# Attention outputs of batches 1 to 7 turned by DMA transposes instead of on TensorE, and four d_ff chunks of a group begun side by side

## The chip, the cores and the metric

One core of a Trainium2 chip runs the whole kernel. It has a TensorE (PE, whose weight loads are listed as PEld), a VectorE (DVE), a ScalarE (ACT), a GpSimd (POOL), a SyncE (SP) that here only issues DMAs, and 16 DMA engines that all queues share. SBUF and PSUM are on the core; inputs and outputs lie in HBM (device memory). The metric is the device time of one launch in microseconds (us): a median of 327.94 us over three runs before the change, from 324.74 to 328.09.

## The reference

The inputs are q, k and v of 8 batches, 8 heads, 576 positions and 64 columns, and two weight matrices of 512 x 2048 and 2048 x 512. The attention of a head is the sum of two parts. Cut to what matters:

```
q_d, k_d, v_d = means of 4 neighbouring positions      # 144 positions
out_up    = repeat(softmax(q_d k_d^T / 8) v_d, 4)        # each of the 144 rows 4 times
out_local = softmax(q k^T / 8 where |i - j| < 4) v
x = (out_up + out_local) as 4608 tokens x 512            # 512 = 8 heads x 64
h = x @ w_in
out = (h * sigmoid(1.702 h)) @ w_out                     # 4608 x 512, float32
```

## The kernel before

**Tokens and groups.** The second half works on nine groups of 512 tokens (`g`, 0 to 8); a batch has 576 tokens, so batch b must be ready when group g = b begins. `xT[hp]`, four tiles of 128 x 4608 in bf16, hold x transposed: tile hp has the 128 columns of the head pair hp in its partitions, and the tokens along the row. `mm1` makes, for each of the 16 chunks of d_ff (`ffc`), four matmuls of 128 x 512, one for each `xT[dmc]` (`hps_mm`, L704), into one PSUM bank; ACT takes the bank to `gT` by a SiLU (L715). `mm2` makes 64 matmuls for a group (L760), 16 for each of four blocks of 128 tokens; ACT scales each block into `osb` and SP stores it (`store`, L745 and L750).

**Attention among the matmuls.** The attention of batch b is computed during group g = b - 1, cut into steps. The lists `POS` and `POS_0` (group 0) name the places: numbers up to 16 count chunks of `mm1`, and from 16 up, matmuls of `mm2` after the first 16. Step by step: scores of half of the heads on PE (`s_pe`), exponentials on ACT (`s_act`), the same for the other half (`s1`), the products with v for head pairs 0 and 1 and for 2 and 3 (`avn`), and two or four steps `tr`. The order of instructions on every engine is the order in the program (a manual schedule); an engine, or SP's queue, that waits for one instruction holds back all that stand behind it.

**A head pair's output.** `av_local` and `av_down` (L445, L467) write the local and the pooled outputs of a pair, with a column of row sums beside each, into a PSUM tile `PA[n]` of two banks. `normalise` divides on DVE (L483, L484) and leaves `y` with queries in the partitions. `transp` turns `y` by 26 small matmuls with the identity for each pair (L498, L508) into another `PA` tile. `copy_od` (ACT, L617) repeats the pooled part four times, and `merge` (DVE, L638 and L644) adds both and writes `xT[hp]`. Batch 0 goes another way, at the head of the program (`av_local0`, `av_down0`, `normalise0`, `transp_sum`, `copy_x`).

**PSUM.** There are eight banks: three `PA` tiles of two and two single banks `PM`. `mm1` and `mm2` of groups 1 to 8 use the two `PM` banks in turn.

**Loads.** SP's queue holds, in program order, for each group: the rows of v for the pooled part (`load_v4`, L245, six DMAs of 192 KB), the rows of v for the local part (`load_v`, L222, ten DMAs of 128 KB), and the group's four stores. POOL issues the loads of q and k (L202), after the additions that pool q and k (`pool_qk`, L309 and L313), which follow the transposes of q and k on DVE (`prep_1`, L279). In group 0 the loads of batch 2 stand in SP's queue ahead of that group's stores, and the first waits until the last part of `w_out_bf` has landed (the `gate`, L796):

```
            load_v(2, gate=after(w_out_bf[0:1, 12, 0:1], nc.gpsimd))
            load_v4(2)
```

Of the kernel before, what the change touches and what calls it, by code (L numbers as in the profile page):

```python
# [8 lines left out]
FP32 = mybir.dt.float32  # L9
BF16 = mybir.dt.bfloat16  # L10
# [9 lines left out]
def kernel(  # L20
# [9 lines left out]
    nc = tc.nc  # L30
# [33 lines left out]
    eds = [persist.tile([128, 2, 464], BF16, name=f"ed{i}") for i in range(2)]  # L64
# [53 lines left out]
    def fill():  # L118
        nc.vector.memset(wz, 0.0)
        for t in kdT:  # L120
            nc.vector.memset(t[:, SD:160, :], 0.0)
        for t in vbs:
            nc.vector.memset(t[:, :, :, 64:65], 1.0)
        for t in vds:
            nc.vector.memset(t[:, :, :, 64:65], 4.0)
        for t in es:
            nc.vector.memset(t[:, :, 300:304], 1.0)
        for t in eds:
            nc.vector.memset(t[:, :, 432:464], 1.0)
# [300 lines left out]
    def av(b, hp, n=None):  # L430
        o = ps_tile(n)
        av_local(b, hp, o)
        av_down(b, hp, o)
        return o

# [3 lines left out]
    def av_local(b, hp, o, chunks=range(5)):  # L439
        E, vb, o = es[hp], vbs[b % 2], banks(o)  # L440
        for i in chunks:
            for par in range(2):
                for j in range(2):
                    pos = j if par == 0 else 1 - j
                    nc.tensor.matmul(  # L445
                        o[par][64 * pos : 64 * pos + 64, 65 * i : 65 * i + 65],
                        lhsT=E[64 * par : 64 * par + 64, j, 60 * i : 60 * i + 64],
                        rhs=vb[64 * par : 64 * par + 64, i, 2 * hp + j, :],
                        start=True, stop=True,
                        tile_position=(64 * par, 64 * pos),  # L450
                    )

    def av_down(b, hp, o):
        Ed, vd, u, o = eds[hp // 2], vds[b % 2], hp % 2, banks(o)

        blocks = [(kc, x, 0) for kc in range(3) for x in range(2)]
        blocks += [(0, 0, 1), (0, 1, 1), (1, 0, 1), (2, 0, 1)]
        if True:
            for kc, x, c2 in blocks:
                for j in range(2):  # L460
                    pos = j if x == 0 else 1 - j
                    c0 = 65 * (5 + c2)
                    q0 = SD * kc + 48 * (min(x + c2, 1) + x)
                    last = x == c2 == 1
                    if last:
                        q0 = 0
                    nc.tensor.matmul(  # L467
                        o[j][64 * pos : 64 * pos + 64, c0 : c0 + 65],
                        lhsT=Ed[64 * j : 64 * j + 48, u, q0 : q0 + 64],
                        rhs=vd[64 * j : 64 * j + 48, kc, hp, :],  # L470
                        start=(kc == 0), stop=(kc == 2 or last),
                        tile_position=(64 * j, 64 * pos),
                    )

    def normalise(o):
        y = work.tile([128, 2, 7, D], BF16, name="y", tag="y", bufs=4)
        rc = work.tile([128, 2, 7, 1], FP32, name="rc", tag="rc")
        for xs in (slice(0, 1), slice(1, 2)) if o is PM else (slice(0, 2),):
            n = xs.stop - xs.start
            ov = (o[xs.start][:, None, :] if o is PM else o)[:, :, 0:455].rearrange(  # L480
                "p x (c e) -> p x c e", e=65
            )
            nc.vector.reciprocal(rc[:, xs], ov[:, :, :, 64:65])  # L483
            nc.vector.tensor_tensor(  # L484
                out=y[:, xs], in0=ov[:, :, :, 0:D],
                in1=rc[:, xs].to_broadcast([128, n, 7, D]), op=ALU.mult,
            )
        return y

    def transp(y, n=None):  # L490
        x = ps_tile(n)
        for i in range(5):
            for par in range(2):
                for j in range(2):
                    pos = j if par == 0 else 1 - j
                    c0 = 0 if (par == 1 or i == 0) else 3
                    c1 = 60 if (par == 0 or i == 4) else 57
                    nc.tensor.matmul(  # L498
                        x[64 * j : 64 * j + 64, par, 57 * i + c0 : 57 * i + c1],
                        lhsT=y[64 * pos : 64 * pos + 60, par, i, :],  # L500
                        rhs=ident(pos, 60, c0, c1),
                        start=True, stop=True,
                        tile_position=(64 * pos, 64 * j),
                    )
        for c2, xx in ((0, 0), (0, 1), (1, 0)):
            for j in range(2):
                pos = j if xx == 0 else 1 - j
                nc.tensor.matmul(  # L508
                    x[64 * j : 64 * j + 64, xx, 288 + 48 * c2 : 336 + 48 * c2],
                    lhsT=y[64 * pos : 64 * pos + 48, j, 5 + c2, :],  # L510
                    rhs=ident(pos, 48, 0, 48),
                    start=True, stop=True,
                    tile_position=(64 * pos, 64 * j),
                )
        return x

    def av_local0(hp, o, chunks):
        E, vb = es[hp], vbs[0]
        for i in chunks:
            for j in range(2):  # L520
                for par in range(2):
# [7 lines left out]
                    )  # L529

# [16 lines left out]
    def y_tiles0():  # L547
        return (
            work.tile([128, 2, 6, D], BF16, name="yl", tag="yl", bufs=4),
            work.tile([128, 2, 2, D], BF16, name="yd", tag="yd", bufs=4),  # L550
            work.tile([128, 2, 7, 1], FP32, name="rc0", tag="rc0", bufs=4),
        )
# [61 lines left out]
    def copy_od(x):  # L614
        od = work.tile([128, S], FP32, name="od", tag="od")
        for xx, t0, n in ((0, 0, 96), (1, 96, 48)):
            nc.scalar.copy(  # L617
                out=od[:, 4 * t0 : 4 * (t0 + n)].rearrange("p (t f) -> p t f", f=4),
                in_=x[:, xx, 288 : 288 + n, None].to_broadcast([128, n, 4]),
            )  # L620
        return od

    def sub(t, off, *dims):
# [3 lines left out]
        )  # L627

    def merge(b, hp, x, od, eng=None):
        t0 = b * S
        eng = eng or nc.vector
        if eng is nc.gpsimd:
            xs = work.tile([128, 2, 512], BF16, name="xs", tag="xs", bufs=2)
            nc.scalar.copy(out=xs[:, :, 0:288], in_=x[:, :, 0:288])
            x = xs
        eng.tensor_tensor(  # L638
            out=sub(xT[hp], t0 + 3, (57, 2), (114, 5), (1, 57)),
            in0=sub(x, 3, (509, 2), (57, 5), (1, 57)),  # L640
            in1=sub(od, 3, (57, 2), (114, 5), (1, 57)),
            op=ALU.add,
        )
        eng.tensor_tensor(  # L644
            out=sub(xT[hp], t0, (573, 2), (1, 3)),
            in0=sub(x, 0, (512 + 285, 2), (1, 3)),
# [312 lines left out]
```

## Time and profile before

| what | value |
|---|---|
| runs | 324.74, 328.09 and 327.94 us, median 327.94 |
| span of the profiled execution, first to last instruction | 324.8 us (the profile gives no time of its own beside it) |
| PE busy | 312.3 us, 96% |
| ACT, POOL and DVE busy | 184.6, 139.2 and 128.1 us |
| of DVE: divisions of `normalise`, L484 | 28 of 1092 ns |
| of DVE: additions of `merge`, L638 and L644 | 28 of 753 ns and 28 of 169 ns |
| of ACT: copies of `copy_od`, L617 | 56, 18.5 us in all |
| PE work of `transp`, L498 and L508 | 728 small matmuls |
| one group with attention, 98.3 to 131.8 us | 33.5 us, PE busy in all of it |
| a group without, 266.2 to 293.9 us | 27.7 us |

Busy times of several engines overlap, so their sum says nothing. What counts is the chain of work that ended last, and which engine an idle stretch waited for. A matmul of 128 x 512 is listed with 379 ns, but matmuls are pipelined: nine in a row start 0.216 us apart.

### The profile page before, as it was taken

How to read it: one execution, taken by the hardware profiler on the slowest of the kernel's cores; microseconds unless marked ns; L12 is line 12 of the kernel's file. 1: busy time of each engine (PE TensorE's matmuls, PEld its weight loads, DVE VectorE, ACT ScalarE, POOL GpSimd, SP SyncE). 2: the span in 40 equal slices, each digit the busy share in tenths (PEclk: the TensorE clock that was granted, in tenths of full speed). 3: DMA queues.
4: the chain of work that ended last, by engine and by line, in shares of the span. 5: the costliest groups of instructions: out<-in, count | busy, mean ns of one | idle time of the engine just before them, and what ended most of it. 6: DMA issues, size and time to landing. Idle time of an engine off the chain costs nothing.

```text
span 324.8 us, 11101 instructions
## 1 busy us (share of the span) xinstructions
PE 312.3 (96%) x4979; PEld 159.9 (49%) x4979; DVE 128.1 (39%) x221; ACT 184.6 (57%) x321; POOL 139.2 (43%) x171
## 2 busy tenths in 40 slices
PE   7669999899999999999999999999999999999995
PEld 4545455445554555455545554455445544444444
DVE  6864524650566037702780178116720660000000
ACT  4443883375846593659266836774677557415611
POOL 8973960089306950596039802990197000000000
PEclk9988999999999999999999999999999999999999
DMA  7999999799717981699149933994290110021012
GB/s 121 124 202 210 159 122 209 152 249 224 143 69 151 208 162 46 157 199 190 38 130 191 179 90 104 184 193 110 71 141 3 69 48 21 0 84 47 0 60 71
DMA packets 63551, 40.04 MB, mean 123 GB/s; under 512 B 44048, under 2 KB 54416, under 8 KB 63504
## 3 DMA queue, kind: packets, MB, share of 16 engines
q1 hardware_dynamic: 44496, 24.32, 34.4%
q0 software_dynamic: 18864, 14.95, 33.3%
q8 instruction: 39, 0.64, 0.9%
q10 hardware_dynamic: 144, 0.07, 0.1%
q14 instruction: 8, 0.07, 0.1%
HBM read 44.83 MB, written 9.44 MB: 167 GB/s over the span
## 4 chain that ended last, share of the span: by engine, by line
PE 92%; DMA 4%; issue 2%; DVE 1%; POOL 1%; ACT 0%; POOLq 0%
PE pm L704 36%; PE pm L760 36%; PE pa L384 3%; PE pa L403 2%; PE pa L760 2%; PE pa L704 2%; DMA qb<-in_q_dram 2%; PE pa L445 2%; PE pa L498 2%; DMA vb<-in_v_dram 2%; PE pa L467 2%; PE pm L775 1%; PE pm L656 1%; PE pa L508 0%; PE pa L523 0%
## 5 line engine op out<-in xcount | busy, mean ns | idle before, releaser
L760 PE MATMUL pm<-w_out_bf,gT 128*128 128x512 bf16 x528 | 121.7, 380 | 0.0
L704 PE MATMUL pm<-xT,w_in_bf 128*128 128x512 bf16 x544 | 121.1, 379 | 0.0
L715 ACT ACTIVATE gT<-pm 128x512 bf16<-128x512 f32 x136 | 81.0, 598 | 45.6 <-PE pm L704 45.6
L704 PEld LDWEIGHTS <-w_in_bf 128*128 128x128 bf16 x576 | 55.6, 98 | 66.7 <-issue 0.7
L760 PEld LDWEIGHTS <-gT 128*128 128x128 bf16 x560 | 51.6, 98 | 58.5 <-issue 0.2
L309 POOL TENSOR_TENSOR pq<-kT 128x576 f32<-128x576 bf16 x14 | 16.2, 1157 | 90.7 <-DVE kT L279 90.6
L428 DVE TENSOR_TENSOR es<-es,mask 128x600 bf16<-128x600 bf16 x28 | 15.2, 542 | 101.1 <-ACT es L414 99.9
L745 ACT ACTIVATE osb<-pm 128x512 f32<-128x512 f32 (+2 forms) x35 | 20.7, 593 | 41.9 <-PE pm L760 37.9
L617 ACT COPY od<-pa 128x384 f32<-128x384 f32 (+1 forms) x56 | 18.5, 411 | 30.8 <-PE pa L508 26.0
L484 DVE TENSOR_TENSOR y<-pa,rc 128x896 bf16<-128x896 f32 x28 | 30.6, 1092 | 1.0
L638 DVE TENSOR_TENSOR xT<-pa,od 128x570 bf16<-128x570 f32 x28 | 21.1, 753 | 11.0 <-ACT od L617 10.2
L325 POOL TENSOR_TENSOR v<-v 112x512 f32<-112x512 f32 x18 | 22.8, 1265 | 0.0
L747 DVE TENSOR_SCALAR osb<-pm 128x128 f32<-128x128 f32 x1 | 0.3, 292 | 55.3 <-ACT osb L745 55.3
L414 ACT ACTIVATE es<-pa 128x600 bf16<-128x600 f32 x32 | 19.9, 685 | 1.2 <-PE pa L384 1.2
L279 DVE STREAM_TRANSPOSE kT<-kb 128x576 f32<-128x576 f32 x16 | 20.0, 1247 | 0.0
L279 DVE STREAM_TRANSPOSE qT<-qb 128x576 f32<-128x576 f32 x16 | 19.8, 1240 | 0.0
L384 PE MATMUL pa<-qT,kT 32*64 32x60 bf16 x1280 | 16.9, 204 | 1.9 <-DVE qT L279 1.2
L233 POOL DMA_DIRECT2D vb<-in_v_dram x20 | 13.7, 700 | 6.5 <-DMA w_in_bf<-in_moe_w_in_dram 4.0
L384 PEld LDWEIGHTS <-kT 32*64 32x64 bf16 x1280 | 15.0, 103 | 2.6 <-issue 2.0
L420 ACT ACTIVATE ed<-pa 128x864 bf16<-128x864 f32 x16 | 14.4, 903 | 2.3 <-PE pa L403 2.2
L309 POOL TENSOR_TENSOR pq<-qT 128x576 f32<-128x576 bf16 x13 | 14.9, 1146 | 0.0
L328 POOL TENSOR_TENSOR vd<-v 112x256 bf16<-112x256 f32 x18 | 13.8, 769 | 1.4
(97 smaller groups left out, 259.1 us busy)
## 6 DMA issues: line engine op xcount, KB each, us to landing
out_dram<-osb SPq DMA_DIRECT2D x35, 256.0 KB, 2.1
vf<-in_v_dram SPq DMA_DIRECT2D x60, 128.0 KB, 5.8
v<-in_v_dram SPq DMA_DIRECT2D x36, 192.0 KB, 5.2
kb<-in_k_dram POOLq DMA_DIRECT2D x16, 288.0 KB, 7.3
qb<-in_q_dram POOLq DMA_DIRECT2D x16, 288.0 KB, 7.8
w_out_bf<-in_moe_w_out_dram POOLq DMA_DIRECT2D x4, 512.0 KB, 9.9
vb<-in_v_dram POOLq DMA_DIRECT2D x20, 64.0 KB, 5.6
w_in_bf<-in_moe_w_in_dram POOLq DMA_DIRECT2D x2, 512.0 KB, 9.2
```

Of the source, the lines that this page charges most:

```text
L279: nc.vector.transpose(out=t32.rearrange("p (i c) -> p c i", c=18), in_=store[b, qd].bitcast(FP32).rearrange("p (c d) -> p c d", c=18),)
L309: nc.gpsimd.tensor_tensor(out=t1, in0=sv[:, :, 0:2, :], in1=sv[:, :, 2:4, :], op=ALU.add)
L325: eng.tensor_tensor(out=t1[0:112], in0=x[:, :, 0:2, :], in1=x[:, :, 2:4, :], op=ALU.add)
L384: nc.tensor.matmul(sp[r // 2][64 * par : 64 * par + 64, r % 2, 60 * i : 60 * i + 60], lhsT=kT[b, qd][rows, k0 : k0 + 64, a], rhs=qT[b, qd] ...
L414: nc.scalar.activation(out=es[2 * qd + u][:, :, 0:300], in_=sp[u][:, :, 0:300], func=AF.Exp, scale=inv_sqrt_d,)
L484: nc.vector.tensor_tensor(out=y[:, xs], in0=ov[:, :, :, 0:D], in1=rc[:, xs].to_broadcast([128, n, 7, D]), op=ALU.mult,)
L617: nc.scalar.copy(out=od[:, 4 * t0 : 4 * (t0 + n)].rearrange("p (t f) -> p t f", f=4), in_=x[:, xx, 288 : 288 + n, None].to_broadcast([128, ...
L638: eng.tensor_tensor(out=sub(xT[hp], t0 + 3, (57, 2), (114, 5), (1, 57)), in0=sub(x, 3, (509, 2), (57, 5), (1, 57)), in1=sub(od, 3, (57, 2) ...
L704: nc.tensor.matmul(acc, lhsT=w_in_bf[:, dmc, ffc * 128 : (ffc + 1) * 128], rhs=xT[dmc][:, g * TG : g * TG + TG], start=(dmc == 0), stop=(d ...
L715: nc.scalar.activation(out=gT[:, ffc, :], in_=acc, func=AF.Silu, scale=GELU_SCALE)
L745: eng.activation(out=osb, in_=ap, func=AF.Copy, scale=1.0 / GELU_SCALE)
L760: nc.tensor.matmul(ops[t], lhsT=gT[:, ffc, t * 128 : (t + 1) * 128], rhs=w_out_bf[:, ffc, :], start=(ffc == 0), stop=(ffc == n_ffc - 1),)
```

## The change

The change has five parts, for batches 1 to 7.

1. `transp` and its steps go. `turn_y` issues one DMA transpose on SP's queue for each head pair: the whole of `y` (128 x 1024, bf16, 256 KB) into an SBUF tile `x` of eight blocks of 128 x 128. That is 28 DMAs.
2. So that whole blocks can be turned, `y` has another layout. `av_local` and `av_down` write other places of the PSUM tile, in the order that batch 0 had, and `normalise` takes one more instruction. Batch 0 keeps its way and shares the new tile `y`.
3. `copy_od` goes. `merge` is three DVE instructions in place of two: a copy of the local part, a copy of six columns, and an addition of the pooled part, which reads each element four times. The merges of all four pairs stand behind the fourth pair's division.
4. The first four chunks of `mm1` in groups 1 to 8 run side by side: `xT[0]` and `xT[1]` for all four, then `xT[2]`, then `xT[3]`. The chunks are spread over all eight PSUM banks.
5. The places of the steps: the second `avn` comes two matmuls earlier in groups 1 to 6, and in group 0 at 60 in place of 64; batch 1 has five steps as the other batches.

SP's queue in the changed program has, in group 0: ten loads of L222, six of L245, the four transposes of batch 1, and then the four stores. In groups 1 to 6: the loads, the store of block 0, two transposes, the store of block 1, two transposes, and the stores of blocks 2 and 3.

```diff
--- before.py
+++ after.py
-    eds = [persist.tile([128, 2, 464], BF16, name=f"ed{i}") for i in range(2)]
+    eds = [persist.tile([128, 2, 480], BF16, name=f"ed{i}") for i in range(2)]
...
-            nc.vector.memset(t[:, :, 432:464], 1.0)
+            nc.vector.memset(t[:, :, 432:480], 1.0)
...
-    def av(b, hp, n=None):
-        o = ps_tile(n)
-        av_local(b, hp, o)
-        av_down(b, hp, o)
-        return o
...
-        blocks = [(kc, x, 0) for kc in range(3) for x in range(2)]
-        blocks += [(0, 0, 1), (0, 1, 1), (1, 0, 1), (2, 0, 1)]
...
-    def transp(y, n=None):
-        x = ps_tile(n)
-        for i in range(5):
-            for par in range(2):
-                for j in range(2):
-                    pos = j if par == 0 else 1 - j
-                    c0 = 0 if (par == 1 or i == 0) else 3
-                    c1 = 60 if (par == 0 or i == 4) else 57
-                    nc.tensor.matmul(
-                        x[64 * j : 64 * j + 64, par, 57 * i + c0 : 57 * i + c1],
-                        lhsT=y[64 * pos : 64 * pos + 60, par, i, :],
-                        rhs=ident(pos, 60, c0, c1),
-                        start=True, stop=True,
-                        tile_position=(64 * pos, 64 * j),
-                    )
-        for c2, xx in ((0, 0), (0, 1), (1, 0)):
...
+    def av_down(b, hp, o):
+        Ed, vd, u = eds[hp // 2], vds[b % 2], hp % 2
+        blocks = [(kc, c) for kc in range(3) for c in (0, 1)]
+        blocks += [(kc, 2) for kc in range(3)] + [(0, 3)]
+        for kc, c in blocks:
+            pos, slot = ((1, 4), (0, 6), (1, 6), (1, 5))[c]
+            for j in range(2):
+                q0 = SD * kc + 64 * (c % 3)
+                nc.tensor.matmul(
+                    o[64 * pos : 64 * pos + 64, j, 65 * slot : 65 * slot + 65],
+                    lhsT=Ed[64 * j : 64 * j + 48, u, q0 : q0 + 64],
+                    rhs=vd[64 * j : 64 * j + 48, kc, hp, :],
+                    start=(kc == 0), stop=(kc == 2 or c == 3),
+                    tile_position=(64 * j, 64 * pos),
+                )
+
+    def normalise(o):
+        y = work.tile([128, 8, 2 * D], BF16, name="y", tag="y", bufs=4)
+        rc = work.tile([128, 2, 7, 1], FP32, name="rc", tag="rc")
+        ov = o[:, :, 0:455].rearrange("p x (c e) -> p x c e", e=65)
+        nc.vector.reciprocal(rc, ov[:, :, :, 64:65])
+        nc.vector.tensor_tensor(
+            out=y[:, 0:6].rearrange("p (x m) (j d) -> p x (m j) d", x=2, j=2),
+            in0=ov[:, :, 0:6, 0:D],
+            in1=rc[:, :, 0:6].to_broadcast([128, 2, 6, D]), op=ALU.mult,
+        )
+        nc.vector.tensor_tensor(
+            out=y[:, 6:8].rearrange("p s (j d) -> p j s d", j=2),
+            in0=ov[:, :, 4:7:2, 0:D],
+            in1=rc[:, :, 4:7:2].to_broadcast([128, 2, 2, D]), op=ALU.mult,
+        )
+        return y
+
+    def turn_y(y):
+        x = work.tile([128, 8, 128], BF16, name="x", tag="x", bufs=4)
+        nc.sync.dma_start_transpose(out=x, in_=y.rearrange("p g c -> p (g c)"))
+        return x
+
+    def merge(b, hp, x):
+        t0 = b * S
+        nc.vector.tensor_copy(
+            out=sub(xT[hp], t0 + 3, (57, 2), (114, 5), (1, 57)),
+            in_=sub(x, 3, (381, 2), (64, 5), (1, 57)),
+        )
+        nc.vector.tensor_copy(
+            out=sub(xT[hp], t0, (573, 2), (1, 3)),
+            in_=sub(x, 0, (384 + 256 + 57, 2), (1, 3)),
+        )
+        xs = xT[hp][:, t0 : t0 + S].rearrange("p (t f) -> p t f", f=4)
+        nc.vector.tensor_tensor(
+            out=xs, in0=xs,
+            in1=sub(x, 832, (1, SD), (0, 4)), op=ALU.add,
+        )
...
+        y = work.tile([128, 8, 2 * D], BF16, name="y", tag="y", bufs=4)
         return (
-            work.tile([128, 2, 6, D], BF16, name="yl", tag="yl", bufs=4),
-            work.tile([128, 2, 2, D], BF16, name="yd", tag="yd", bufs=4),
+            y[:, 0:6].rearrange("p (x m) (j d) -> p x (m j) d", x=2, j=2),
+            y[:, 6:8].rearrange("p s (j d) -> p s j d", j=2),
             work.tile([128, 2, 7, 1], FP32, name="rc0", tag="rc0", bufs=4),
...
-    def copy_od(x):
-        od = work.tile([128, S], FP32, name="od", tag="od")
-        for xx, t0, n in ((0, 0, 96), (1, 96, 48)):
-            nc.scalar.copy(
-                out=od[:, 4 * t0 : 4 * (t0 + n)].rearrange("p (t f) -> p t f", f=4),
-                in_=x[:, xx, 288 : 288 + n, None].to_broadcast([128, n, 4]),
-            )
-        return od
...
-    def merge(b, hp, x, od, eng=None):
...
-        eng.tensor_tensor(
-            out=sub(xT[hp], t0 + 3, (57, 2), (114, 5), (1, 57)),
-            in0=sub(x, 3, (509, 2), (57, 5), (1, 57)),
-            in1=sub(od, 3, (57, 2), (114, 5), (1, 57)),
-            op=ALU.add,
-        )
...
-    def attention(b, slots=None):
+    def attention(b):
         st = {}
+        slot = (1, 2, 1, 2) if b == 1 else (0, 1, 2, 0)
 
         def s_pe(qd):
-            t = PA if b == 1 else [ps_tile() for _ in range(3)]
-            st["d", qd] = scores_d(b, qd, t[0])
-            st["s", qd] = scores(b, qd, sp=t[1:3])
+            st["d", qd] = scores_d(b, qd, PA[0])
+            st["s", qd] = scores(b, qd, sp=PA[1:3])
 
         def s_act(qd):
             if qd == 0:
@@ -681,24 +621,16 @@
         def avn(*hps):
             def f():
                 for hp in hps:
-                    st["o", hp] = av(b, hp, slots and slots[hp % 2])
+                    av_local(b, hp, PA[slot[hp]])
+                    av_down(b, hp, PA[slot[hp]])
                 for hp in hps:
-                    st["y", hp] = normalise(st["o", hp])
+                    st["x", hp] = turn_y(normalise(PA[slot[hp]]))
+                if hps[-1] == HP - 1:
+                    for hp in range(HP):
+                        merge(b, hp, st["x", hp])
             return f
 
-        def tr(*hps):
-            def f():
-                for hp in hps:
-                    st["x", hp] = transp(st["y", hp], slots and slots[hp % 2])
-                for hp in hps:
-                    od = copy_od(st["x", hp])
-                    merge(b, hp, st["x", hp], od)
-            return f
-
-        first = [lambda: s_pe(0), lambda: s_act(0), s1, avn(0, 1)]
-        if b == 1:
-            return first + [tr(0), tr(1), avn(2, 3), tr(2), tr(3)]
-        return first + [avn(2, 3), tr(0, 1), tr(2, 3)]
+        return [lambda: s_pe(0), lambda: s_act(0), s1, avn(0, 1), avn(2, 3)]
...
-    def mm1(g, gT, steps, first=0):
-        for ffc in range(first, n_ffc):
+    def mm1(g, gT, steps):
+        half = [PA[n][:, u, :] for n in (1, 2, 0) for u in range(2)]
+        bank = [PM[0], *half[0:4], PM[1], *half[4:6]]
+        bank += [PM[0], half[0], half[1], PM[1]] + PM + PM
+        if g == 0:
+            bank = acc[0:6] + late
+        for ffc in range(n_ffc):
             for f in steps.get(ffc, ()):
                 f()
-            hps = pm_tile() if g else acc[ffc] if ffc < 6 else late[ffc - 6]
-            for dmc in range(n_dmc):
-                hps_mm(g, ffc, dmc, hps)
-            silu(gT, ffc, hps)
+            if g and ffc < 4:
+                if ffc == 0:
+                    for dmcs in ((0, 1), (2,), (3,)):
+                        for u in range(4):
+                            for dmc in dmcs:
+                                hps_mm(g, u, dmc, bank[u])
+            elif g or ffc > 5:
+                for dmc in range(n_dmc):
+                    hps_mm(g, ffc, dmc, bank[ffc])
+            else:
+                continue
+            silu(gT, ffc, bank[ffc])
 
     def mm2(g, gT, steps):
         tok0 = g * TG
+        turn["m"] = 1
...
-    POS = [13, 16, 33, 42, 53, 62, 71]
-    POS_0 = [16, 18, 27, 46, 50, 55, 64, 68, 73]
+    POS = [13, 16, 33, 42, 51]
+    POS_0 = [16, 18, 27, 46, 60]
...
-            for n, f in zip(POS if g else POS_0, attention(b, None if g else (1, 2))):
+            for n, f in zip(POS if g else POS_0, attention(b)):
...
-        mm1(g, gT, steps, 0 if g else 6)
+        mm1(g, gT, steps)
```

## The prediction

> **What bounds the kernel now.** I read the page's busy times and chain first, then PE's order of time in one steady group, then SP's queue, because the new DMAs go there.
>
> ```profile
> PE 312.3 (96%) x4979; PEld 159.9 (49%) x4979; DVE 128.1 (39%) x221; ACT 184.6 (57%) x321; POOL 139.2 (43%) x171
> ...
> PE 92%; DMA 4%; issue 2%; DVE 1%; POOL 1%; ACT 0%; POOLq 0%
> ```
>
> PE is the bound, so only PE time and new PE waits count; the 18.5 us of ACT copies that go (L617) lie on no chain and are worth nothing. The end of group 2 on PE:
>
> ```profile
> 124.50 2.12 PE L760 MATMUL pm<-w_out_bf,gT 128*128 128x512 bf16 x9
> 126.55 0.35 PE L498 MATMUL pa<-id,y 60*64 60x60 bf16 x20
> 126.73 0.22 PE L508 MATMUL pa<-id,y 48*64 48x48 bf16 x6
> ...
> 127.10 2.12 PE L760 MATMUL pm<-w_out_bf,gT 128*128 128x512 bf16 x9
> ...
> 129.70 2.12 PE L760 MATMUL pm<-w_out_bf,gT 128*128 128x512 bf16 x9
> 131.66 1.67 PE L704 MATMUL pm<-xT,w_in_bf 128*128 128x512 bf16 x7
> ```
>
> Nine matmuls take 9 x 0.2157 = 1.94 us (a 52-matmul stretch of the chain takes 11.22), so the step `tr` between 124.50 and 127.10 costs 2.60 - 1.94 = 0.66 us, the next one as much, and group 3 starts without a wait. SP's queue in group 0:
>
> ```profile
> 53.24 9.77 SPq L222 DMA_DIRECT2D vf<-in_v_dram  x10
> 63.05 3.06 SPq L245 DMA_DIRECT2D v<-in_v_dram  x6
> 66.23 3.64 SPq L750 DMA_DIRECT2D out_dram<-osb  x4
> ```
>
> The sixteen loads of batch 2 hold the queue until 66.1, after PE has begun group 1 (64.53). The four stores behind them show what a 256 KB DMA meets there, against the median of all stores (the listing for 66 to 70 us, then the page):
>
> ```profile
> out_dram<-osb SPq DMA_DIRECT2D x4, 256.0 KB, 6.5
> ```
>
> ```profile
> out_dram<-osb SPq DMA_DIRECT2D x35, 256.0 KB, 2.1
> ```
>
> **Gain.** For batches 2 to 7, two steps of 0.66 go: 6 x 1.32 = **7.9 us**. In group 0 the four `tr` steps cost 1.96 (gaps of 0.44, 0.43, 0.66 and 0.43), but PE will wait at its end for something that does not depend on them, so I count nothing.
>
> **AV products.** As many matmuls, other order, which batch 0 already has: its 20 L539 took 0.34 us from first load to the next group, 20 L467 took 0.33. I take 0.01 x 28 = **+0.3**. Bounds: nothing to 0.13 a pair (the loads alone, 0.30 against 0.17), 3.6.
>
> **DVE.** Batch 0 has the new division's shapes:
>
> ```profile
> 22.58 0.25 DVE L558 RECIPROCAL rc<-pa 128x14 f32<-128x14 f32 x1 [1.90 <-PE pa L539]
> 22.86 0.42 DVE L560 TENSOR_TENSOR yd<-pa,rc 128x256 bf16<-128x256 f32 x1
> 23.20 0.95 DVE L565 TENSOR_TENSOR yl<-pa,rc 128x768 bf16<-128x768 f32 x1
> ```
>
> 22.58 to 24.15 is 1.57 us a pair, before 1.28. A merge is now two SBUF bf16 passes over about 570 elements and one over six. The mask multiply (L428, SBUF bf16, 600 elements) takes 0.542, so I take 0.54 + 0.54 + 0.12 = 1.2 us. Bounds: 0.88 (the copy at half of it, the small one at 0.07 as the smallest memsets) and 1.67 (two L638 of 0.753 and an L644 of 0.169).
>
> **Steady boundaries (groups 1 to 6).** Let T be the first division, 120.96 in group 2. PE resumes at 121.20, does 9 matmuls, AV (0.93, as in this group) and 29 matmuls: the new group begins at 121.20 + 1.94 + 0.93 + 6.26 = T + 9.37. Side-by-side chunks give 8 matmuls from `xT[0]` and `xT[1]`, then 4 from `xT[2]`, so `xT[3]` is wanted at T + 11.96. Four divisions end at T + 6.28, four merges at T + 11.1: in time by 0.9 us. The fourth turn is issued at T + 6.4 and must land within 11.96 - 6.4 - 1.2 = 4.4 us. The trace has no transpose; a store of equal size lands in 2.1, a v load among its fellows in 5.8. I take 2.1, the nearest in size and quiet: DMAs are idle in most of 121 to 131 us. Cost nothing, covered by those 12 matmuls. At 5.8 it is 1.4 us a boundary, 8.4 in all; at the merge bound of 1.67, merges end at T + 12.96, 1.0 a boundary.
>
> The Trainium skill, "Advanced Engine Details and Errata", section X-Bar Transpose (TRN2), says that these DMAs are as fast as regular ones; by that the 2.1 stands. No run shows it.
>
> **Boundary 0 to 1.** Without its `tr` steps PE ends group 0 at about 62. The turns of batch 1 stand behind the sixteen loads, so the first goes out at 66.2, into rings that are still full: the last v load there, issued at 65.67, took 6.9 us and landed at 72.6, and the first store, issued at 66.23, at 73.3. With a turn in the store's place I take 72.6, since the next q and k loads (POOL, 69.81) now wait behind the merges. Merges end at 73.8, 75.0, 76.2, 77.4; the stores' spacing of 0.8 keeps the later turns ahead of them. PE has then stood still for 11 us, and its clock drops:
>
> ```profile
> 20.00:21.00 1.00, 0.00 (x0) 0.00 (x0) 0.68 (x2) 0.99 (x2) 0.69 (x1) 1.00 1.24 204
> ...
> 23.00:24.00 1.00, 1.00 (x4) 0.40 (x3) 1.00 (x2) 0.00 (x0) 0.80 (x2) 0.50 1.13 213
> 24.00:25.00 1.00, 1.00 (x16) 0.65 (x14) 0.15 (x1) 0.00 (x0) 0.65 (x1) 0.50 1.12 213
> 25.00:26.00 1.00, 1.00 (x44) 0.88 (x43) 0.11 (x1) 0.85 (x3) 0.00 (x0) 0.50 1.12 216
> ```
>
> (granted clock third from the end: about 3.3 us at 0.50 after a pause of some 2 us). So seven matmuls of 0.43 run from 75.0 to 78.0, one more at 0.43, seven at 0.216: the first sixteen end at 79.95. Before, 64.53 + 16 x 0.2157 = 67.98. **Loss 12.0 us.** Without the clock's fall 77.4 + 0.86 = 78.3, loss 10.3; with a first landing as the last one among vf (4.1 after 66.2), 9.7; with one at 2.1, merges of 0.88 and full clock, 68.3 + 3.5 + 0.86, loss 4.7. Behind it queue only DVE's transposes for batch 2, 12 us later, and POOL's chain behind them: 19.4 us from DVE's start to the last `vd` (98.61 to 118.04), wanted some 20 us after the last merge, so just covered. The delayed stores have four `osb` tiles and are wanted a group later.
>
> **Sum.** -7.9 + 0.3 + 12.0 = **+4.4 us**. Span 324.8 becomes 329.2; the page has no own time for the execution, and the lowest run equals the span, so I add to the median: 327.94 + 4.4 = **332.3 us**.
>
> **Rivals.**
> - Slow turns: each lands too late at every boundary as well. For it: DMA rows with 256-byte pieces take 5.8; a queue of four turns at the v loads' rate (1.28 MB in 10.5 us, 2.1 us each) ends at T + 10.1, on the edge. Against: quiet DMAs. 4.4 + 8.4 gives 340.7.
> - Short wait: the rings empty sooner and boundary 0 loses about 7.6, half-way in its bounds: 327.9. Against it speak the four stores' 6.2 to 7.3 us.
> - Faster: the loads of v are out of the way, and the turns hide in group 0 too: -7.9 - 1.96 + 0.3 gives 318.4. It decides if `xT[3]` of batch 1 is whole by about 65. The queue's order speaks against it. That the turns don't replace the matmuls is excluded: the changed program has 28 of them and no L498.
> - A turn by blocks: eight blocks of 128 x 128 one after another, each with the smallest store's landing of 1.6 us, make 12.8 a turn, 51 a batch, more than a group; 66 + 7 x 51 + 58 is 481 us. Against: no DMA row behaves so. The Trainium skill, "VectorE: DVE Perf Modes", section The three transpose paths, gives 1309 ns for such a block against 390 on TensorE; by that a turn would be 10.5 us, by estimate, and the time about 418. No run shows it.
>
> **Chances.** Forecast 0.52 (329 to 335), slow turns 0.22, short wait 0.16, faster 0.08, by blocks 0.02. The measurement tells about 1% from no change, 3.3 us. Of the forecast, 0.40 lies above 331.2 and 0.12 below; short wait gives 0.13 same and 0.03 faster. So faster 0.11, same 0.25, slower 0.64. The range is 326 to 342.5: it leaves out faster and by blocks, and some of slow turns and of short wait.
>
> **What would show it.** No L498 and L508; 128 plain matmuls and 33.5 - 1.3 = 32.2 us in groups 2 to 6 without a PE wait at their starts; in group 0 four transposes on SP at 66 to 70 us, PE idle from about 62 to 74 for DVE's merge, clock 0.50 after it. Wrong if a quiet turn takes over 4.4 us, or if PE waits under 8 us at 62.

## The result, and the profile after

The changed kernel takes **357.63 us** (median of four runs, 356.58 to 359.24), the kernel before 327.43 us beside it (324.74 to 328.09). The ratio is **1.095**, with a 95% interval of 1.088 to 1.102: slower by some 30 us, where +4.4 us were forecast and 342.5 us was the upper end of the range. The profiled execution took 357.70 us, its span is 355.8 us; so a run is its span and 1.9 us, and the span has grown by 31.0 us from 324.8. Medians here and below are over all runs of a kernel; ratios and their intervals leave out the few runs that lay over 1.5% above the kernel's fastest.

The page of the kernel after, first its busy times, then the shares of the chain by engine:

```profile
PE 309.2 (87%) x4251; PEld 154.0 (43%) x4251; DVE 140.8 (40%) x277; ACT 164.1 (46%) x265; POOL 138.4 (39%) x171
...
PE 68%; DMA 8%; ACT 7%; DVE 5%; POOL 4%; SPq 3%; issue 3%; ACTq 0%; POOLq 0%; DVEq 0%
```

PE has the 728 small matmuls less, as the change says, and it is no longer busy all the time: 96% became 87%. On the chain DMA has 8% for 4%, and ACT, which had 0% before, now has 7% of it. ACT itself works less than before (164 for 185 us), so its 7% can't come from its load; something waits for it. The two longest rows of PE's waits say what (line waited for: us in total, times, longest):

```profile
PE pa L636 <- ACT gT L647: 23.4, 24, 1.6
PE pm L636 <- DVE xT L496: 12.4, 2, 11.8
```

The second row is the wait at the end of group 0 that the prediction had. The first is nowhere in the prediction: matmuls of `mm1` (L636) wait for the SiLU (L647), 24 times. In order of time they stand here, in group 3 on PE (start, us, line, operation, count, and in brackets the idle time ahead of it):

```profile
148.87 0.81 PE L636 MATMUL pa<-xT,w_in_bf 128*128 128x512 bf16 x3
149.76 0.38 PE L636 MATMUL pm<-xT,w_in_bf 128*128 128x512 bf16 x1
149.97 0.81 PE L636 MATMUL pa<-xT,w_in_bf 128*128 128x512 bf16 x3
152.35 1.02 PE L636 MATMUL pa<-xT,w_in_bf 128*128 128x512 bf16 x4 [1.56 <-ACT gT L647]
153.21 1.03 PE L636 MATMUL pm<-xT,w_in_bf 128*128 128x512 bf16 x4
154.07 1.03 PE L636 MATMUL pa<-xT,w_in_bf 128*128 128x512 bf16 x4
155.78 1.02 PE L636 MATMUL pa<-xT,w_in_bf 128*128 128x512 bf16 x4 [0.69 <-ACT gT L647]
...
159.22 1.02 PE L636 MATMUL pa<-xT,w_in_bf 128*128 128x512 bf16 x4 [0.69 <-ACT gT L647]
```

and this is ACT in the same microseconds:

```profile
150.73 1.57 ACT L647 ACTIVATE gT<-pa 128x512 bf16<-128x512 f32 x3
...
154.27 0.60 ACT L647 ACTIVATE gT<-pm 128x512 bf16<-128x512 f32 x1 [0.27 <-PE pm L636]
155.14 0.60 ACT L647 ACTIVATE gT<-pa 128x512 bf16<-128x512 f32 x1 [0.27 <-PE pa L636]
```

Three matmul chunks of a group wait, always the same ones. Counted from 0 they are chunks 4, 7 and 10. In the table of banks they are `PA[2]` second half, `PA[0]` second half and `PA[1]` second half, and the chunk just ahead of each has the first half of the same tile. The wait ends when ACT has read that first half: at 152.30 (150.73 + 1.57) ends the SiLU of chunk 3, at 152.35 begins chunk 4; at 155.74 (155.14 + 0.60) ends that of chunk 6, at 155.78 begins chunk 7. Chunk 4 and chunk 3 lie in two different banks; but both are halves of one tile, and the program holds the wait for the whole tile. Its order of instructions on PE shows it: the first matmul of chunk 4 waits for an ACT instruction,

```
Matmult pa2_98<-xT0_79,w_in_bf_77 128x512 [waits Activation_49]
```

and so do the first ones of chunks 7 and 10. Chunks 13 to 15 carry such a wait too, each for the chunk two before it in the same `PM` bank, and chunk 0 one for its bank's last use in the group before; none of these appears among PE's waits, which are the 24 at chunks 4, 7 and 10. Chunk 2 also follows the other half of its tile, but its matmuls stand ahead of all SiLUs of the first four chunks, so it has nothing to wait for.

By the starts of the matmuls a wait costs a little more than the row lists: four matmuls in a row take 0.86 us (152.35 to 153.21). From 149.97 to 152.35, less three matmuls of 0.216, are 1.73; from 154.07 to 155.78, less 0.86, are 0.85, and the third is as long. That is 3.43 us a group, and in the eight groups 1 to 8 **27.4 us** of the 31.0 by which the span grew.

The boundary from group 0 to group 1, on SP's queue:

```profile
50.96 9.77 SPq L222 DMA_DIRECT2D vf<-in_v_dram  x10
60.77 3.05 SPq L245 DMA_DIRECT2D v<-in_v_dram  x6
63.94 8.09 SPq L482 DMA_TRANSPOSE x<-y  x4
72.13 2.01 SPq L696 DMA_DIRECT2D out_dram<-osb  x4
```

and on PE:

```profile
58.01 1.89 PE L706 MATMUL pa<-w_out_bf,gT 128*128 128x512 bf16 x8
71.70 0.61 PE L636 MATMUL pm<-xT,w_in_bf 128*128 128x512 bf16 x1 [11.80 <-DVE xT L496]
72.93 0.58 PE L636 MATMUL pm<-xT,w_in_bf 128*128 128x512 bf16 x1 [0.62 <-DVE xT L496]
...
78.00 1.06 PE L636 MATMUL pa<-xT,w_in_bf 128*128 128x512 bf16 x3
```

The four turns of batch 1 stand behind the sixteen loads of batch 2, the first goes out at 63.94 and lands 6.4 us later, PE stands from 59.9 to 71.7, and the first sixteen matmuls of group 1 end at 78.9. Before, they ended at 67.98: a loss of 10.9 us. The clock falls too, in the windows of two microseconds (the granted clock is the third number from the end):

```profile
66.00:68.00 2.00, 0.00 (x0) 0.00 (x0) 0.00 (x0) 0.00 (x0) 0.00 (x0) 0.50 1.14 192
...
74.00:76.00 2.00, 2.00 (x6) 0.72 (x5) 1.93 (x5) 0.00 (x0) 0.00 (x0) 0.50 1.00 379
...
78.00:80.00 2.00, 1.06 (x4) 0.38 (x3) 1.75 (x2) 1.70 (x4) 1.92 (x3) 0.88 0.00 0
```

The account of the span goes by the ends of the first sixteen matmuls of a group. Groups 1 and 7 start on PE before in the first two rows, group 7 after in the third:

```profile
64.53 11.48 PE L704 MATMUL pm<-xT,w_in_bf 128*128 128x512 bf16 x52
...
266.09 13.98 PE L704 MATMUL pm<-xT,w_in_bf 128*128 128x512 bf16 x64
```

```profile
289.93 0.59 PE L636 MATMUL pm<-xT,w_in_bf 128*128 128x512 bf16 x2
```

Before, from 67.98 in group 1 to 269.54 in group 7 (start 266.09 + 16 x 0.2157) are 201.6 us; after, from 78.9 to 293.4 (start 289.93) 214.5 us, 12.9 more. In them lie 6 x 3.43 = 20.6 us of waits, so the rest of these six groups became 7.7 us shorter. With the boundary and all waits that is 10.9 + 27.4 - 7.7 = 30.6 of the 31.0.

### The profile page after: what moved, and what is told of

It reads as the page before. It is cut to its first block, busy times and chain, and to the rows that moved or that the text cites. A ratio compares the mean times of both kernels' runs of the same rounds, so it can differ in the third digit from the quotient of the medians.

```text
span 355.8 us, 9677 instructions
## 1 busy us (share of the span) xinstructions
PE 309.2 (87%) x4251; PEld 154.0 (43%) x4251; DVE 140.8 (40%) x277; ACT 164.1 (46%) x265; POOL 138.4 (39%) x171
## 2 busy tenths in 40 slices
DMA packets 93114, 47.29 MB, mean 133 GB/s; under 512 B 73616, under 2 KB 83984, under 8 KB 93072
## 4 chain that ended last, share of the span: by engine, by line
PE 68%; DMA 8%; ACT 7%; DVE 5%; POOL 4%; SPq 3%; issue 3%; ACTq 0%; POOLq 0%; DVEq 0%
PE pm L706 26%; PE pm L636 16%; PE pa L636 16%; ACT gT L647 6%; DMA x<-y 4%; SPq L222 3%; DMA w_out_bf<-in_moe_w_out_dram 3%; PE pa L384 2%; DMA qb<-in_q_dram 2%; PE pa L403 2%; PE pa L439 2%; POOL vb L233 2%; DVE y L468 1%; PE pa L455 1%; DVE xT L496 1%
## 5 line engine op out<-in xcount | busy, mean ns | idle before, releaser
L706 PE MATMUL pm<-w_out_bf,gT 128*128 128x512 bf16 x528 | 119.1, 379 | 0.0
L636 PEld LDWEIGHTS <-w_in_bf 128*128 128x128 bf16 x576 | 56.0, 99 | 110.7 <-issue 37.0
L636 PE MATMUL pa<-xT,w_in_bf 128*128 128x512 bf16 x288 | 75.7, 387 | 23.4 <-ACT gT L647 23.4
L636 PE MATMUL pm<-xT,w_in_bf 128*128 128x512 bf16 x288 | 73.3, 383 | 12.5 <-DVE xT L496 12.4
L706 PEld LDWEIGHTS <-gT 128*128 128x128 bf16 x560 | 52.8, 98 | 61.9 <-issue 0.5
L647 ACT ACTIVATE gT<-pm 128x512 bf16<-128x512 f32 x72 | 42.8, 599 | 59.3 <-PE pm L636 59.3
L428 DVE TENSOR_TENSOR es<-es,mask 128x600 bf16<-128x600 bf16 x28 | 13.2, 472 | 112.9 <-ACT es L414 111.7
L647 ACT ACTIVATE gT<-pa 128x512 bf16<-128x512 f32 x72 | 41.0, 602 | 31.5 <-PE pa L636 31.5
L468 DVE TENSOR_TENSOR y<-pa,rc 128x768 bf16<-128x768 f32 x28 | 26.8, 957 | 1.0
L496 DVE TENSOR_TENSOR xT<-xT,x 128x576 bf16<-128x576 bf16 x28 | 21.2, 758 | 1.0
L487 DVE COPY xT<-x 128x570 bf16<-128x570 bf16 x28 | 8.8, 315 | 17.5 <-DMA x<-y 17.3
```

The lines of the kernel that those rows point to most:

```text
L468: nc.vector.tensor_tensor(out=y[:, 0:6].rearrange("p (x m) (j d) -> p x (m j) d", x=2, j=2), in0=ov[:, :, 0:6, 0:D], in1=rc[:, :, 0:6].to_ ...
L496: nc.vector.tensor_tensor(out=xs, in0=xs, in1=sub(x, 832, (1, SD), (0, 4)), op=ALU.add,)
L636: nc.tensor.matmul(acc, lhsT=w_in_bf[:, dmc, ffc * 128 : (ffc + 1) * 128], rhs=xT[dmc][:, g * TG : g * TG + TG], start=(dmc == 0), stop=(d ...
L647: nc.scalar.activation(out=gT[:, ffc, :], in_=acc, func=AF.Silu, scale=GELU_SCALE)
L706: nc.tensor.matmul(ops[t], lhsT=gT[:, ffc, t * 128 : (t + 1) * 128], rhs=w_out_bf[:, ffc, :], start=(ffc == 0), stop=(ffc == n_ffc - 1),)
```

## The experiments

Two explanations stand against each other for the 27 us. The theory: the waits come from the spreading over PSUM banks alone, because halves of one `PA` tile follow one another; other banks take them all away, and another order of the chunks does not. The rival: ACT is late at these places, since the four SiLUs of the side-by-side chunks come in one bunch; then other banks leave waits, and chunks one after another take them away. All diffs are against the kernel after.

### Other banks

```diff
-        bank = [PM[0], *half[0:4], PM[1], *half[4:6]]
-        bank += [PM[0], half[0], half[1], PM[1]] + PM + PM
+        bank = [PM[0], *half[0:3], PM[1], half[4]]
+        bank += [PM[0], half[0], half[2], half[4]] + PM + PM + PM
```

The first four chunks run side by side as after; no half follows the other half of its tile, except in these four.

> The changed kernel with another list of PSUM banks for mm1, so that no chunk goes into the second half of a two-bank tile PA while ACT still has to read the first half; nothing else differs. Theory: the three PE waits for ACT in each of groups 1 to 8 (1.56, 0.69 and 0.69 us listed; by the starts of the matmuls 1.73 + 0.84 + 0.84 = 3.41 us a group) come from the wait for the other half of the same tile. Then all 24 waits go and the time falls by about 8 x 3.41 = 27 us, to 330. Rival: ACT is late because four SiLUs fall due at once after the side-by-side chunks; then a wait of 1 to 2 us a group stays at the fifth chunk and the time falls by no more than 14 us, to 344 or more.

Measured: 331.13 us against 326.81 before, ratio 1.014 (1.008 to 1.021); 26.5 us less than the kernel after. PE's order of time in group 3, behind the side-by-side chunks:

```profile
142.72 1.03 PE L636 MATMUL pm<-xT,w_in_bf 128*128 128x512 bf16 x4
143.59 1.03 PE L636 MATMUL pa<-xT,w_in_bf 128*128 128x512 bf16 x3
144.45 1.03 PE L636 MATMUL pm<-xT,w_in_bf 128*128 128x512 bf16 x4
145.31 2.75 PE L636 MATMUL pa<-xT,w_in_bf 128*128 128x512 bf16 x12
```

There is no bracket in it: chunk after chunk starts 0.86 us behind the one before (a matmul record is missing in the second row). No wait for L647 is left on PE; the longest is that of batch 1:

```profile
PE pm L636 <- DVE xT L496: 12.2, 2, 11.6
```

The theory holds and the rival falls: the tile that two chunks share is the cause, and not ACT's bunch of SiLUs. With this undone the kernel is 331.1 - 326.8 = 4.3 us slower than before, and the forecast for the whole was 4.4. In its profiled execution the first sixteen matmuls of group 1 end at 77.2, 9.2 us later than before, and those of group 7 at 272.2, so groups 1 to 6 became 6.6 us shorter (195.0 for 201.6).

### The same banks, the chunks one after another

```diff
-            if g and ffc < 4:
-                if ffc == 0:
-                    for dmcs in ((0, 1), (2,), (3,)):
-                        for u in range(4):
-                            for dmc in dmcs:
-                                hps_mm(g, u, dmc, bank[u])
-            elif g or ffc > 5:
+            if g or ffc > 5:
```

This separates the two things that the change's fourth part does at once: the order of the first four chunks, and the table of banks.

> The changed kernel with its own list of banks, but the first four chunks of a group one after another instead of side by side. Theory of the shared tile: a wait of about 0.85 us at each second half of a tile, now chunks 2, 4, 7 and 10, so 3.4 us a group as before; and xT[3] is wanted 0.65 instead of 2.59 us after a group's start, where the last merge ends some 3.0 us after it: 2.1 us more at six boundaries. Together about 357.6 + 12.6 = 370 us. Rival (four SiLUs at once): the waits for ACT go, -27 + 12.6, about 343 us.

Measured: 368.88 us, ratio 1.130 (1.124 to 1.136). PE's waits:

```profile
PE pa L636 <- ACT gT L647: 21.9, 32, 0.7
PE pm L636 <- DVE xT L496: 21.3, 15, 12.3
```

and chunks 2 and 3, then chunk 4, in group 3:

```profile
155.29 1.89 PE L636 MATMUL pa<-xT,w_in_bf 128*128 128x512 bf16 x8 [0.69 <-ACT gT L647]
157.86 1.02 PE L636 MATMUL pa<-xT,w_in_bf 128*128 128x512 bf16 x4 [0.69 <-ACT gT L647]
```

The waits do not go with the bunch, as the rival had it. Chunk 2 waits as well now, as the theory asks: four waits a group, 32 in all. Each has about 0.69 us, the one at chunk 4 too, since no bunch of SiLUs stands ahead of it. And the second row, 12.4 in 2 after, is 21.3 in 15: with the chunks one after another PE wants `xT[2]` and `xT[3]` earlier than they are merged.

### The turns alone

```diff
-        bank = [PM[0], *half[0:4], PM[1], *half[4:6]]
-        bank += [PM[0], half[0], half[1], PM[1]] + PM + PM
+        bank = PM * 8
```

and the chunks one after another, as in the experiment before. Banks and order are those of the kernel before; the turns, the divisions, the merges and the places of the steps are those of after.

> The turns without the other half of the change: chunks one after another and in the two PM banks in turn, as before the change; batches 1 to 7 by DMA. Theory: no wait for ACT, but xT[3] wanted 0.65 us after a group's start, where the last merge ends some 3 us after it: six boundaries of about 2.1 us more than in the banks-apart kernel, 331.1 + 12.6 = 343.7 us. Rival: the turns land early enough for the merges in all groups but the first, and side-by-side chunks are worth nothing: 331 to 333 us.

Measured: 342.98 us against 326.94, ratio 1.053 (1.047 to 1.059). The longest waits (none for L647 is among them), and the wait for `xT[3]` at the start of group 3 on PE:

```profile
PE pm L636 <- DVE xT L496: 19.5, 14, 10.4
```

```profile
146.04 10.78 PE L636 MATMUL pm<-xT,w_in_bf 128*128 128x512 bf16 x49 [0.85 <-DVE xT L496]
```

With the first two experiments and the kernel after this makes a table of two by two (medians):

| | chunks side by side | one after another |
|---|---|---|
| halves behind halves | 357.6 (after) | 368.9 |
| no halves behind halves | 331.1 | 343.0 |

The two kernels without halves behind halves have different tables of banks: the one of 331.1 us uses six banks, the one of 343.0 the two `PM` banks in turn. The order is worth 11.3 and 11.9 us, the banks cost 26.5 and 25.9: to within 0.6 us the two parts add up. So the side-by-side order does what the prediction asked of it (12 matmuls that cover the merges), and the turns without it lose 16 us.

### Batch 1 by the old way

For the boundary of group 0 the question is whether the 10.9 us come from the turns' place in SP's queue. Here the turns of batch 1 are not made at all: it goes on TensorE, with the functions and the nine steps of the kernel before, and only batches 2 to 7 are turned by DMA. The banks are those of the first experiment.

```diff
+        if b == 1:
+            return first + [avn_pe(0, 1), tr(0), tr(1), avn_pe(2, 3), tr(2), tr(3)]
+        return first + [avn(0, 1), avn(2, 3)]
...
-    POS_0 = [16, 18, 27, 46, 60]
+    POS_0 = [16, 18, 27, 46, 50, 55, 64, 68, 73]
```

> The banks-apart kernel with batch 1 turned on TensorE as before the change (its own steps and places), batches 2 to 7 by DMA. Theory: boundary 0 to 1 then costs nothing (the first 16 matmuls of group 1 end at about 68 as before, against 77.2 in the banks-apart kernel), and what is left is 1.32 us a group for six groups, less 0.25 at each start where the last merge is late: 327 - 7.9 + 0.3 + 1.5, about 321 us, 2% faster than the kernel before. Rival: some of the gain of the banks-apart kernel came out of the long pause (queues run empty in it), and without it turns meet full rings in the later groups; then 325 us or more.

Measured: **321.27 us against 326.94 before, ratio 0.981 (0.976 to 0.986)**: 1.9% less than the kernel before. PE at the end of group 0:

```profile
62.91 1.69 PE L835 MATMUL pa<-w_out_bf,gT 128*128 128x512 bf16 x7
64.44 0.59 PE L765 MATMUL pm<-xT,w_in_bf 128*128 128x512 bf16 x2
...
101.90 1.03 PE L765 MATMUL pm<-xT,w_in_bf 128*128 128x512 bf16 x4
...
134.07 1.03 PE L765 MATMUL pm<-xT,w_in_bf 128*128 128x512 bf16 x4
```

Group 1 begins at 64.4 as it did before (64.53), without a wait, and a steady group takes 32.2 us (the same `PM` chunk at 101.90 in group 2 and 134.07 in group 3); two of the six take about 1 us more, with pauses of PE in the AV products that the trace puts to nothing. From the first experiment's 331.1 to this are 9.9 us, close to the 9.2 that its trace gives for the boundary and the 10.9 of the kernel after.

### The loads behind the turns

The other way to free the boundary: batch 1 is turned by DMA, but the loads of batch 2 go into SP's queue behind its four turns, and without their gate. Banks as in the first experiment.

```diff
-            load_v(2, gate=after(w_out_bf[0:1, 12, 0:1], nc.gpsimd))
-            load_v4(2)
...
+        if g == 0:
+            steps.setdefault(POS_0[-1], []).append(lambda: (load_v(2), load_v4(2)))
```

> The banks-apart kernel with the sixteen loads of v for batch 2 issued on SP behind the four turns of batch 1 instead of ahead of them. Theory (the turns are held by what stands ahead of them in their own queue): the turns go out at 54 to 59 us, meet only the last q and k loads of POOL's queue, and the first 16 matmuls of group 1 end at 67 to 69 instead of 77.2; the loads land by 78, in time for POOL: 322 us. Rival (any other traffic on the DMA engines holds a turn back, as with the loads on POOL's queue, where a turn took up to 20.9 us): the turns land late again, at 68 us or after, 328 us or more.

Measured: 322.18 us, ratio 0.989 (0.983 to 0.995), 1.1% less than before. SP's queue and PE's starts:

```profile
53.12 8.03 SPq L482 DMA_TRANSPOSE x<-y  x4
61.20 6.81 SPq L222 DMA_DIRECT2D vf<-in_v_dram  x10
```

```profile
61.22 0.38 PE L636 MATMUL pm<-xT,w_in_bf 128*128 128x512 bf16 x1 [0.28 <-DVE xT L496]
...
63.68 0.38 PE L636 MATMUL pm<-xT,w_in_bf 128*128 128x512 bf16 x1 [0.79 <-DVE xT L496]
```

The same four transposes, 11 us earlier; the two landings that the trace gives took 4.8 and 5.3 us, group 1 begins at 60.56, and its first sixteen matmuls end at 65.8, two microseconds ahead of the kernel before. So the turns of batch 1 do hide in group 0 when no loads stand ahead of them; those loads make the loss. Whether they do so by holding SP's queue or by filling the DMA engines, this run does not tell.

### The loads on another queue

The same aim by a smaller edit: the sixteen loads keep their place in the program, but POOL issues them in place of SP (banks as in the first experiment).

```diff
-                nc.sync.dma_start(
+                (nc.gpsimd if b == 2 else nc.sync).dma_start(
```

(in `load_v` and in `load_v4`)

> As the banks-apart kernel, and the sixteen loads of v for batch 2 are issued from POOL's queue instead of SP's. Theory: the turns of batch 1 waited 6 to 8 us for SP's queue, and for the DMA rings that those loads had filled; now they go out as soon as y is there, at 54 to 59 us, and xT[3] of batch 1 is whole by about 66 instead of 75.3 us: 8 to 12 us less than the banks-apart kernel, about 320. Rival: the DMA engines, not the queue, hold the turns back; then they land no earlier than 68 to 72 us and the time falls by under 4 us.

Measured: 341.33 us, ratio 1.044 (1.037 to 1.051): 10 us slower than with the loads on SP. My theory that the wait for the queue is all of it fell here. The turns now go out from 54.2, but look at their landing, in the listing of DMAs for 50 to 80 us, and at DVE's merges:

```profile
x<-y SPq DMA_TRANSPOSE x4, 14.6
```

```profile
60.95 0.32 DVE L487 COPY xT<-x 128x570 bf16<-128x570 bf16 x1 [0.85 <-DMA x<-y]
...
67.65 0.32 DVE L487 COPY xT<-x 128x570 bf16<-128x570 bf16 x1 [5.38 <-DMA x<-y]
...
75.96 0.32 DVE L487 COPY xT<-x 128x570 bf16<-128x570 bf16 x1 [6.90 <-DMA x<-y]
```

A turn that took 3.3 us in a quiet stretch takes a median of 14.6 and at worst 20.9 us while the loads of the other queue run beside it, and the fourth merge comes at 82.4. It ends 8.4 us later than in the banks-apart kernel (83.7 for 75.3), which is most of the 10 us. The Trainium skill ("DMA: Bandwidth & Descriptors", Issuing engines are not separate DMA queues) says that transfers of all issuers run on the same 16 DMA engines and interleave there; this run agrees. Three runs of the same four transposes: behind the loads of their own queue they land in 3.1 to 6.4 us, ahead of them in 4.8 to 5.3, beside loads of another queue in 6.7 to 20.9.

### Matmuls to keep the clock

After the wait PE's clock is at 0.50. Would matmuls without a use, in the wait, save what that costs? Banks as in the first experiment, and at the end of group 0's `mm2`:

```diff
+        if g == 0:
+            warm(52, t=PM[1])
```

> As the banks-apart kernel, and 52 matmuls of 128 x 512 without use (about 11.2 us at full clock) fill PE's wait at the end of group 0. Theory: the granted clock of 0.50 after the wait costs 2 to 3 us at the start of group 1 (the first 16 matmuls ended at 78.9, the last merge at 75.3); with the clock held at 1.00 they end 0.9 after the last merge, so 2.5 us less than the banks-apart kernel. Rival: the merges alone set the end there and nothing changes, within 0.5 us.

Measured: 334.18 us, ratio 1.019 (1.010 to 1.028). The four runs spread from 330.4 to 336.8, those without the matmuls from 329.7 to 331.5, and the intervals of the two ratios overlap. In the profiled execution group 0 itself ended late (66.4 for 60.0), and the 52 matmuls ended at 77.6, two microseconds behind the last merge (75.7): they were in the way. The first sixteen of group 1 then took 3.45 us, as at full clock, but began 6 us later than without the 52, so the run does not tell what the clock costs. With 42:

> The banks-apart kernel with 42 matmuls without use (9.1 us at full clock) in PE's wait at the end of group 0, so that they end before the first merge (71.6); 52 of them ended after the merges and proved nothing. Theory: the fall of the granted clock costs the start of group 1 about 1.1 us (first 16 matmuls end at 77.2, last merge at 75.2, four matmuls at full clock take 0.86): 330 against 331.1. Rival: no difference at all, if the drop is only while PE waits for merges anyway.

Measured: 334.07 us, ratio 1.016 (1.010 to 1.022). Its windows (clock third from the end):

```profile
74.00:76.00 2.00, 0.51 (x2) 0.20 (x2) 1.93 (x5) 0.00 (x0) 0.00 (x0) 0.86 1.07 198
76.00:78.00 2.00, 2.00 (x6) 0.65 (x5) 1.86 (x6) 0.00 (x0) 0.00 (x0) 0.50 1.05 382
```

The matmuls ended at 71.7, PE stood for another 2.9 us, and the clock fell to 0.50 all the same, in the window from 76 on. The six runs spread from 329.4 to 335.5, and the interval of the ratio overlaps with that of the banks-apart kernel (1.008 to 1.021). So neither number of matmuls shows a gain, and a loss is not shown either; what the clock is worth here was not measured by itself. The banks-apart kernel gives a hint: its last merge ends at 75.3 as in the kernel after, but its clock is back sooner: 0.74 as the mean of these ten microseconds, so at 0.50 until about 75.2,

```profile
70.00:80.00 10.00, 7.74 (x29) 3.15 (x30) 9.15 (x16) 3.04 (x6) 3.32 (x4) 0.74 0.63 173
```

and the first sixteen matmuls end at 77.2 for 78.9, 1.1 us behind what the merges allow (75.3 + 0.86) in place of 2.7. The same pause costs different amounts in two executions.

## Why the prediction was wrong

- **The step that failed** stands under steady boundaries: the side-by-side chunks were counted as "Cost nothing, covered by those 12 matmuls", and the forecast of a steady group as 32.2 us without a wait followed from it. The order of the chunks was costed, the spreading over the eight banks was not, though it is the same part of the change. It cost 3.43 us in each of eight groups, 27.4 us. Two lines of the kernel show it without any time: the table of banks with two halves of a `PA` tile behind one another, and a SiLU in between. No rival had it, and the range had no room for it.
- **Gain, 7.9, and AV products, +0.3.** About right: together 7.6, where groups 1 to 6 gained 7.7 without the waits by the sum above, and 6.6 in the banks-apart kernel, where nothing has to be subtracted. A steady group takes 35.59 us (fifth chunks at 152.35 and 187.94), less 3.43 of waits 32.16, for 32.2. The two terms are not shown apart.
- **DVE.** The sums were right, the terms not all. The division takes 0.238 + 0.957 + 0.414, with the gaps a spacing of 1.48 us, for 1.57. The merges follow one another by 1.23 us, for 1.2; but the copy takes 0.32 where 0.54 was counted, the addition 0.76 for 0.54, and the six columns 0.17 for 0.12. The errors took one another away.
- **Turn landing, 2.1.** Too low, and harmless. From the rows of the tile `x` after (issue on SP, in ns; then us from issue to landing):

```profile
L482 SPq DMA_TRANSPOSE x<-y x28: 1232/1286/3908, 63.9 to 287.8; - x28
...
DMA to landing us min/median/max: 3.1/3.3/6.4
```

  The fourth turns of the six steady groups landed in 3.2 to 3.9 us, under the 4.4 that the boundaries allow, so they were covered; first turns took up to 5.2, but nothing waits for those so early. The Trainium skill ("Advanced Engine Details and Errata", X-Bar Transpose (TRN2)) says that these DMAs are as fast as regular ones. That is not quite borne out: a store of the same 256 KB has a median of 2.4 us in the same execution.
- **Boundary 0 to 1, loss 12.0.** 10.9 was measured. The mechanism is the one forecast: the turns behind sixteen loads, the wait for L496, the clock at 0.50. PE stood 11.8 us for the 11 forecast. The first turn went out 2.3 us earlier (63.94 for 66.2) and took 6.4 us, as forecast from its neighbours (72.6 - 66.2). At full clock the first sixteen matmuls would have ended 0.86 us behind the last merge of 75.34, at 76.2; 78.9 is 2.7 us later, for 1.7 forecast. That part is worked out, not shown by a run, and it was 1.1 in the banks-apart kernel, whose boundary lost 9.2.
- **The rivals.** Slow turns fell: PE's waits name `xT` twice, both at the start of group 1; in group 3 the last four of the first sixteen matmuls begin 0.24 us late (149.76, where three matmuls behind 148.87 make 149.52), and that is all. By blocks fell: eight blocks land in 3.3 us together. The Trainium skill ("VectorE: DVE Perf Modes", The three transpose paths) has 1309 ns for one block of 128 x 128, and here it is 0.41 us a block in a turn of eight. Faster (turns hidden in group 0 too, 318.4) did not happen in this kernel, because of the loads ahead in the queue, as the prediction said; with the loads behind the turns the time comes nearer to it (322.2).
- **The direction** was right, and the forecast of +4.4 us is what the kernel does with other banks (+4.3). That is the sum without its missing term, but the match to 0.1 us is luck: the boundary lost 9.2 for 12.0 there and the groups gained 6.6 for 7.6. It does not make the forecast right for the kernel that was asked about.

## What to carry to other kernels

When a change gives work more buffers, cost the wait of each buffer as well as the new order: list which tile each piece writes, who reads that tile last, and whether anything stands between. Two halves of one tile count as one tile in the program's waits, even where they are two banks, so a double tile gives side-by-side work only to pieces whose readers come after both. And a transfer that a critical step waits for belongs ahead of loads in its own queue; moving those loads to another queue was no substitute here.

## What the runs showed of the hardware

- One transpose of 128 x 1024 bf16 takes SP 1.29 us to issue (a store of 256 KB takes about 0.5: four in 2.01), and in a quiet stretch 3.1 to 3.3 us to land. It is cut into 1056 packets, all under 512 B: of such packets the page before (first row) lists 44048 and the page after 73616, 29568 more for 28 turns:

```profile
DMA packets 63551, 40.04 MB, mean 123 GB/s; under 512 B 44048, under 2 KB 54416, under 8 KB 63504
```

```profile
DMA packets 93114, 47.29 MB, mean 133 GB/s; under 512 B 73616, under 2 KB 83984, under 8 KB 93072
```

- That it takes 14.6 us in the middle and 20.9 at worst beside loads of POOL's queue was not expected; that small packets take turns with the larger ones of the loads would explain it, but no run shows it.
- After a pause of 11.8 us with few matmuls behind it, the granted clock stayed at 0.50 until about 78.5 us, nearly seven microseconds after the first matmul, though a continuous run of matmuls began at 73.3. In the banks-apart kernel, with a pause of 11.6 us and the same start, it was back at about 75.2; after the pause of some 2 us shown in the prediction it took 3.3.
- Whether PE could write one bank of a `PA` tile while ACT reads the other without harm was not tried with the waits taken out; the experiments with other tiles make it unnecessary.
